# Twelve first-softmax maxima taken apart between ScalarE, GpSimd and VectorE, and some output matmuls moved between the fill pairs

## The chip, the cores and the metric

The kernel runs on one core of a Trainium2 chip. Its engines work side by side and meet at semaphores: TensorE (PE; its weight loads are listed apart as PEld), VectorE (DVE), ScalarE (ACT), GpSimd (POOL) and SyncE (SP, which here only issues DMAs). [...] The metric is the device time of one execution in microseconds; lower is better.

## The reference

An attention through 32 inducing points over 4 batches of 12416 rows of 128 values, and then a gated feed-forward layer on all 49664 rows:

```
def mab(q, kv):
    s = scale * (q @ kv.T)
    a = exp(s - s.max(-1))
    a /= a.sum(-1) + 1e-9
    return a @ kv
h = mab(inducing, x)        # first softmax: 32 rows over 12416 positions, per batch
y = mab(x, h)               # second softmax: 12416 rows over 32 positions, per batch
out = (sigmoid(y @ w_gate) * (y @ w_val)) @ w_out     # 128 -> 1536 -> 128
```

## The kernel before

**Shapes.** A batch is 97 pieces of 128 rows: six groups of 16 pieces and one piece alone. The hidden width of 1536 is 12 chunks `j` of 128. A block is four pieces (512 rows); one last block takes the four single pieces of the four batches. So there are 97 blocks of 12 chunks.

**The feed-forward layer.** The output of the second softmax is never formed. Its weights `a2` (32 per row) are multiplied at once with `hw = h @ w`, so a gate or value chunk is one matmul with 32 rows of contraction and 512 columns (a fill). Chunks go through *steps* of two and one chunks in turn; two steps are a *slot* of three chunks, and slots number the work of the whole kernel: 96 to a batch. In a step, `product(t)` (L964) has TensorE fill the values of step t and the gates of step t+2, and VectorE forms `u = (tanh + 1) * value` (L981); `gate(t + 2)` (L958) has ScalarE take tanh of the gates (L962). The PSUM tags are `g2, g1, v2, v1` (two- and one-chunk gates and values, one buffer each, six banks), `acc` and `m`. So the value fill of a step waits for VectorE's product two steps earlier, and the gate fill for ScalarE's tanh two steps earlier. `project` (L1050) sends output matmuls (L1062: 128 x 128, four a chunk) into `acc` from a queue, 12 a slot, or 16 while a block that starts with 24 or more waiting is under way; they stand at the end of the slot, behind both fill pairs. When a block is done ScalarE scales it into SBUF (L1081) and SP stores it.

**Beside it.** While batch b is in the feed-forward layer, the first softmax of batch b+1 and the second softmax of later groups run at slots that are written out by hand: `at(slot, make, late)` puts a piece of work behind the slot's first step (late False) or its second (late True), and `beside` (L1130) runs it. All of it shares the one PSUM bank `m`.

- First softmax, `plan_stage1` (L332), a group of 16 pieces: score matmuls into `m` (L255), the maximum over 512 columns by VectorE (L267), exponential by ScalarE one slot later (L280), transposition of the weights by a DMA on SP's queue, weighted sums on TensorE (L315) some slots later, and a copy of the sum (L330).
- `plan_combine` joins the seven groups of a batch with their maxima (GpSimd, with short VectorE and TensorE steps) and makes `hw`.
- Second softmax, `plan_stage2` (L617), a group: 16 small score matmuls into `m` (L483) in two slots, copy to SBUF by ScalarE (L520), `s2_lower_pool` on GpSimd (row maxima by a tree of subtract, clamp at zero, add: L530 to L532; then a subtraction, L535), exponential by ScalarE (L544), sums, inverse and spread on GpSimd (L552 to L598), and a DMA transposition.
- In the last batch nine chunks (`ASIDE`) bypass VectorE: gate and value are filled into `m` (L1015), ScalarE takes tanh and copies the value (L1025, L1029), and GpSimd forms the product (L1026, L1031). Their output matmuls stand at the end of their block.

Loads of x are issued on GpSimd's queue, their DMA transpositions, the output stores and the transpositions of weights on SP's. A prologue runs batch 0's first softmax before the loop.

Of the kernel before, what the change touches and what calls it, by code (L numbers as in the profile page):

```python
# [17 lines left out]
P = 128  # L18
GC = 16
BC = 4  # L20
ASIDE = {3: ((2, 9, 3, 8), (11, 17, 7, 1), (23, 26, 7, 0), (50, 53, 15, 3), (58, 62, 19, 11), (64, 69, 19, 10), (73, 76, 20, 5), (78, 81, 23, 11), (83, 88, 23, 10))}
LATE = (4, 19, 32, 46, 43)
# [15 lines left out]
def kernel(  # L38
# [31 lines left out]
    up = ctx.enter_context(tc.tile_pool(name="up", bufs=6))  # L70
    tp = ctx.enter_context(tc.tile_pool(name="tp", bufs=4))
    op = ctx.enter_context(tc.tile_pool(name="op", bufs=4))
# [145 lines left out]

    summed = [0] * B
    def keep_on(n, tag):  # L220
# [11 lines left out]
    def at(slot, make, late=False, side=False):  # L232
        plan.setdefault((slot, "side" if side else late), []).append(make)
# [15 lines left out]
    def s1_score_pe(b, s, tag, s1=None):  # L249
        c0, n = groups[s]  # L250
        ng, w, R = s1_dims(s)
        if s1 is None:
            s1 = ps.tile([P, 512], F32, tag=tag, name="s1_ps")
# [35 lines left out]
    def s1_turn_pe(b, s, a1T, tag="m"):  # L289
        ng, w, R = s1_dims(s)  # L290
        aT = ps.tile([P, 4, P], F16, tag=tag, name="aT_ps")
# [15 lines left out]
    def s1_sum_pe(b, s, a1, hp, k0, k1):  # L307
        c0, n = groups[s]
# [23 lines left out]
    def plan_stage1(b, s, score, total):  # L332
# [15 lines left out]
        at(score, begin)  # L348
        at(score + 1, weigh, late=full)
        at(score + 2, turn)  # L350
        first, second, keep = total

        def part(k0, k1):
            if k0 == 0:
                st["hp"] = ps.tile([P, C + 1], F32, tag="m", name="hp_ps")
# [4 lines left out]
        at(keep, lambda: s1_sum_keep(b, s, st["hp"]))  # L360
# [21 lines left out]
    def hw_fill(b, hf, tag):  # L382
        hw_ps = ps.tile([P, NI // 2, P], F32, tag=tag, name="hw_ps")
# [32 lines left out]
    def plan_combine(b, lead, weights, fill):  # L416
# [36 lines left out]
        def total():  # L453
            lh = ps.tile([P, 2, m], F32, tag="m", name="lh_ps")
# [4 lines left out]
        def part(hf):  # L459
            st["hw_ps"] = hw_fill(b, hf, "m")  # L460

        def keep(hf):
            if hf == 0:
                st["hwt"] = bp.tile([P, NI, P], F16, tag="hw", bufs=B, name="hwt")
            nc.scalar.copy(out=st["hwt"][:, ts(hf, NI // 2), :], in_=st["hw_ps"][:])
            if hf == 1:
# [724 lines left out]
```

## Time and profile before

| | before |
|---|---|
| median of 3 runs | 719.89 us (719.73 to 719.92) |
| span of the profiled execution | 718.4 us; the median is 1.5 us longer, for what lies around the span |
| mean granted TensorE clock | 0.999 |
| L267, maxima over 512 columns | 22 and 2 more, 683 ns each; six of them in the prologue |
| L962, tanh | 385 of 1024 columns at 1035 ns, 385 of 512 at 609 ns |
| L981, products | 385 of 1024 columns at 1214 ns, 384 of 512 at 679 ns |
| L280, exponentials of the first softmax | 22 at 683 ns and some smaller |

A row of the groups gives line, engine, operation, tiles, shapes and count, then busy time and mean duration of one, then the engine's idle time just before them and what ended it. Durations of neighbours on an engine overlap a little, so the spacing of starts is shorter than the mean duration.

### The profile page before, as it was taken

To read this page: it belongs to the slowest core of one execution; us is meant where nothing else is said; L and a number is where in the kernel's file an instruction comes from. 1 tells how busy PE (TensorE), PEld (TensorE's weight loads), DVE (VectorE), ACT (ScalarE), POOL (GpSimd) and SP (SyncE) were. 2 spreads that over 40 slices of the span, in tenths; PEclk is the share of its full clock that TensorE was granted. 3 is DMA by queue.
4 is the path that set the end of the run, shared out by engine and by line. 5 is a ranking of instruction groups with operands and counts; after the bars stand their busy time and mean duration, and the time that the engine had idled before them with its cause. 6 is when DMAs were issued, how large, how long until landed. Compare 5 with 4: busy or idle time off the path is not lost.

```text
span 718.4 us, 21566 instructions
## 1 busy us (share of the span) xinstructions
PE 650.5 (91%) x8446; PEld 394.2 (55%) x8446; DVE 702.4 (98%) x872; ACT 675.1 (94%) x1019; POOL 445.8 (62%) x718
## 2 busy tenths in 40 slices
PE   8889889999998998999989988999899999999897
PEld 4455555555555555555555555555555555555555
DVE  5899999999999999999999999999999999999997
ACT  4699999999999999999999999999999999999996
POOL 4574763888653747588666266387766787676220
PEclk9999999999999999999999999999999999999999
DMA  9796696244568344335268431220222122223011
GB/s 209 115 182 130 125 165 105 75 90 106 89 133 162 80 103 92 59 79 119 66 117 161 102 75 51 70 74 31 77 60 73 46 62 67 39 75 71 35 46 46
DMA packets 118182, 65.77 MB, mean 92 GB/s; under 512 B 101408, under 2 KB 102208, under 8 KB 118080
## 3 DMA queue, kind: packets, MB, share of 16 engines
q1 hardware_dynamic: 112176, 50.90, 31.6%
q0 software_dynamic: 5584, 13.34, 10.9%
q8 instruction: 66, 1.08, 0.6%
q14 instruction: 36, 0.29, 0.1%
q10 hardware_dynamic: 320, 0.15, 0.1%
HBM read 27.80 MB, written 25.43 MB: 74 GB/s over the span
## 4 chain that ended last, share of the span: by engine, by line
PE 51%; ACT 24%; DVE 16%; issue 5%; DMA 2%; DVEq 1%; POOL 1%; ACTq 0%
PE acc_ps L1062 24%; ACT t L962 22%; PE v_ps L944 21%; DVE u L981 14%; PE g_ps L944 2%; DMA xn<-in_x_dram 2%; PE s_ps L483 2%; PE hp_ps L315 1%; ACT o L1081 1%; DVE nm L267 1%; DVEq L981 1%; ACT a1T L280 0%; PE s_ps L255 0%; POOL xn L96 0%; ACTq L962 0%
## 5 line engine op out<-in xcount | busy, mean ns | idle before, releaser
L981 DVE SCALAR_TENSOR_TENSOR u<-t,v_ps 128x1024 f16<-128x1024 f16 (+1 forms) x771 | 670.9, 945 | 1.7 <-PE g_ps L944 0.8
L962 ACT ACTIVATE t<-g_ps 128x1024 f16<-128x1024 f32 (+1 forms) x770 | 589.5, 822 | 22.2 <-ACT t L962 10.3
L944 PE MATMUL v_ps<-a2r,hwt 32*128 32x512 f16 (+1 forms) x1179 | 290.8, 371 | 56.9 <-DVE u L981 53.2
L1062 PE MATMUL acc_ps<-wo,u 128*128 128x128 f16 x4620 | 324.5, 220 | 0.9
L1062 PEld LDWEIGHTS <-u 128*128 128x128 f16 x4620 | 259.9, 98 | 89.5 <-issue 88.1
L944 PE MATMUL g_ps<-a2r,hwt 32*128 32x512 f16 (+1 forms) x1179 | 294.0, 376 | 0.0
L944 PEld LDWEIGHTS <-hwt 32*128 32x128 f16 x2382 | 93.5, 91 | 188.6 <-issue 142.2
L552 POOL TENSOR_TENSOR sum<-e 128x256 f32<-128x256 f16 (+1 forms) x23 | 15.5, 672 | 133.8 <-ACT e L544 130.0
L598 POOL TENSOR_TENSOR a2n<-e,rs 128x2048 f16<-128x2048 f16 (+3 forms) x25 | 86.8, 3474 | 4.8 <-DVE rs L570 3.1
L576 POOL TENSOR_TENSOR near<-sme,minus 128x16 f32<-128x16 f32 (+1 forms) x22 | 65.3, 2966 | 1.8
L1081 ACT ACTIVATE o<-acc_ps 128x512 f32<-128x512 f32 x96 | 58.4, 609 | 0.0
L531 POOL TENSOR_SCALAR rise<-rise 128x256 f32<-128x256 f32 (+6 forms) x110 | 51.2, 466 | 9.7
L532 POOL TENSOR_TENSOR top<-top,rise 128x128 f32<-128x128 f32 (+3 forms) x88 | 28.4, 323 | 7.3
L552 POOL TENSOR_TENSOR sum<-sum 128x128 f32<-128x128 f32 (+3 forms) x92 | 28.4, 309 | 7.2
L530 POOL TENSOR_TENSOR rise<-top 128x128 f32<-128x128 f32 (+3 forms) x88 | 27.3, 310 | 6.9
L530 POOL TENSOR_TENSOR rise<-sc 128x256 f32<-128x256 f32 (+1 forms) x22 | 16.3, 739 | 20.9 <-ACT sc L520 20.6
L1031 POOL TENSOR_TENSOR xn_spare<-xn_spare 128x512 f16<-128x512 f32 x9 | 11.4, 1270 | 22.2 <-ACT xn_spare L1029 22.0
L535 POOL TENSOR_TENSOR sc<-sc,top 128x512 f32<-128x512 f32 (+1 forms) x22 | 23.9, 1086 | 1.7
L1026 POOL TENSOR_SCALAR xn_spare<-xn_spare 128x512 f32<-128x512 f16 x9 | 13.4, 1493 | 11.2 <-ACT xn_spare L1025 11.2
L483 PEld LDWEIGHTS <-xT 128*128 128x128 f16 x388 | 13.1, 96 | 11.7 <-issue 11.3
L280 ACT ACTIVATE a1T<-s_ps,nm 128x512 f16<-128x512 f32 (+1 forms) x26 | 16.4, 630 | 3.1 <-DVE nm L267 3.0
L483 PE MATMUL s_ps<-hT,xT 128*128 128x32 f16 x388 | 18.1, 178 | 0.1
(150 smaller groups left out, 291.4 us busy)
## 6 DMA issues: line engine op xcount, KB each, us to landing
out_dram<-o SPq DMA_DIRECT2D x96, 256.0 KB, 2.2
xn<-in_x_dram POOLq DMA_DIRECT2D x18, 512.0 KB, 7.7
xn<-in_x_dram POOLq DMA_DIRECT2D x3, 544.0 KB, 6.9
xn<-in_x_dram POOLq DMA_DIRECT2D x3, 256.0 KB, 12.8
xn<-in_x_dram SPq DMA_DIRECT2D x1, 576.0 KB, 4.8
xn<-in_x_dram SPq DMA_DIRECT2D x1, 512.0 KB, 3.9
a2r<-a2n SPq DMA_TRANSPOSE x29, 4.5
wg<-in_moe_w_gate_dram POOLq DMA_DIRECT2D x1, 384.0 KB, 12.7
```

Of the source, the lines that this page charges most:

```text
L483: nc.tensor.matmul(s2[:, j, :], xT[b][:, c + j, :], hT16[b][:], start=(j == 0), stop=whole and j == j1 - 1, skip_group_check=True,)
L530: nc.gpsimd.tensor_tensor(out=r, in0=far, in1=near, op=ALU.subtract)
L531: nc.gpsimd.tensor_scalar_max(out=r, in0=r, scalar1=0.0)
L532: nc.gpsimd.tensor_tensor(out=top[:, 0:n, 0:w], in0=near, in1=r, op=ALU.add)
L552: nc.gpsimd.tensor_tensor(out=d[:, 0:n, :], in0=src[:, :, 0:w], in1=src[:, :, w : 2 * w], op=ALU.add)
L576: nc.gpsimd.tensor_tensor(out=near[:, 0:n], in0=sme[:, 0:n], in1=minus1[:, 0:n], op=ALU.pow)
L598: eng.tensor_tensor(out=a2n[:, 0:n, :, :], in0=e.unsqueeze(2).to_broadcast((P, n, 4, m)), in1=rs.unsqueeze(2).unsqueeze(3).to_broadcast((P ...
L944: st[what + "end"] = nc.tensor.matmul(pt[:, k, col : col + nb * P], hw[b][r : r + 32, j // 2, :], a2r[r : r + 32, o : o + nb, :].rearrange ...
L962: st["tanh"] = nc.scalar.activation(out=st["t"][:], in_=st["g"][:], func=AF.Tanh, scale=0.5)
L981: u = nc.vector.scalar_tensor_tensor(out=st["u"][:, :, c:e], in0=st["t"][:, :, c:e], scalar=1.0, in1=st["v"][:, :, c:e], op0=ALU.add, op1= ...
L1062: nc.tensor.matmul(acc[0][(i // 2) % len(acc[0])][:, i, :], u[:, ts(i, P)], wo16[:, j, :], start=(i in fresh), stop=not any(e[2] == ib and ...
L1081: nc.scalar.mul(out=o32[:], in_=acc[0][0][:], mul=0.5)
```

## The change

**Maxima.** A first-softmax group whose row in the new table `TIMES` has two more slots goes another way. Its scores are filled into `m` at the first slot; late in the same slot ScalarE copies them negated to SBUF (`neg`) and GpSimd folds them by three levels of minimum (`lower_tree`: 512 to 256, 128, 64 columns, three instructions a level). At the second slot VectorE takes the minimum of the last 64 columns, at the third ScalarE takes the exponential from `neg` with scale -1. The other groups go as before. All slots of both softmaxes come from `TIMES` now (first batch, the two middle ones, last): many have moved by some slots, among them transposing loads of x for two groups to 15 and 12 slots before their batch.

**Output matmuls.** Behind the slot's first step, and so ahead of its second fill pair, up to three output matmuls (`GAP`; four in a block at the faster pace) are issued, if a block is under way and nothing else was put on TensorE in that slot so far. The slot still has 12, or 16 in the fast pace, which begins at 28 waiting (20 for blocks 81 and 93).

**The rest.** The chunks left out for the side path are always the last of their block, steps run across block ends, and four of the 18 side fills stand at other places in the slot. Buffers: `up` 6 to 4, `tp` and `op` 4 to 3, and a new pool for `neg`, `low` and the side tiles. The names `BEHIND`, `DROPPED` and `SWAP` are empty and switch nothing.

```
+GAP = 3
+BRISK = (81, 93)
+TIMES = (
+    {
+        "late": {2: (6, 7, 13, None), 3: (18, 19, 27, None), 4: (31, 33, 45, None), 5: (56, 57, 65, 52)},
+        "sum": ((10, 19, 22, 35, 35, 35), (13, 40, 41, 41), (25, 33, 37, 48, 49, 50), (37, 51, 51, 51), (42, 48, 49, 55, 55, 55), (45, 54, 54, 54), (22, 27, 27, 30)),
+        "join": (57, 61, (76, 78), (81, 83)),
+        "next": ((73, 74, 81), (86, 87, 94)),
+        "turn": (3, 7, 16, 21, 31, 37, 12),
+    },
+    {
+        "late": {2: (0, 3, 18, None), 3: (16, 21, 34, None), 4: (36, 37, 50, None), 5: (56, 57, 65, 52)},
+        "sum": ((9, 17, 17, 34, 35, 35), (13, 18, 26, 47, 48, 49), (-6, 3, 6, 50, 51, 51), (29, 35, 39, 45, 46, 46), (-3, 23, 24, 25), (31, 42, 42, 54, 55, 55), (39, 42, 43, 43)),
...
+        "turn": (0, 4, -15, 20, -12, 22, 30),
+    },
+    {
+        "late": {2: (4, 6, 14, None), 3: (19, 21, 29, None), 4: (32, 34, 42, None), 5: (46, 48, 56, 43)},
+    },
+)
+LOW = 64
...
+    def lower_tree(low, neg):
+        w, src = 2 * P, neg
+        rise1 = s2p.tile([P, (GC + NLO) * (m // 2)], F32, tag="sum16", name="rise1")
+        top1 = s2p.tile([P, (GC + NLO) * (m // 2)], F32, tag="sum16", name="top1")
+        while w >= LOW:
+            near, far = src[:, 0:w], src[:, w : 2 * w]
+            r = rise1[:, 0:w]
+            nc.gpsimd.tensor_tensor(out=r, in0=near, in1=far, op=ALU.subtract)
+            nc.gpsimd.tensor_scalar_max(out=r, in0=r, scalar1=0.0)
+            dst = low if w == LOW else top1
+            nc.gpsimd.tensor_tensor(out=dst[:, 0:w], in0=near, in1=r, op=ALU.subtract)
+            src = dst
+            w //= 2
...
+        def leave():
...
+            nc.scalar.mul(out=st["neg"][:], in_=st["s1"][:], mul=-1.0)
+            side_done()
+            lower_tree(st["low"], st["neg"])
+
+        def finish():
+            nm, _, col = s1_col(b, s)
+            nc.vector.tensor_reduce(
+                out=nm[:, col], in_=st["low"][:], axis=AX.X, op=ALU.min
+            )
...
+        if len(total) > 3:
+            done, weight, *total = total
+            at(score, fill)
+            at(score, leave, late=True)
+            at(done, finish)
+            at(weight, weigh_low, late=True)
+            at(weight + 1, turn)
...
         if t % 2 == 0:
             beside(t // 2, False)
+            early = 0
+            gap = BC if brisk or behind else GAP
+            if gap and acc[0] is not None and used == tensor_uses[0]:
+                early = len(queue)
+                project(t - 1, t, min(gap, waiting(t - 1) - 1, block_left() - 1))
+                early -= len(queue)
         else:
             beside(t // 2, True)
-            ready = waiting(t - 1)
+            room = 3 * BC - early if behind or not brisk else 3 * BC
             if acc[0] is None:
-                pace = 4 * BC if ready >= 6 * BC else 3 * BC
-            project(t - 1, t, pace)
+                brisk = waiting(t - 1) >= (5 if queue and queue[-1][2] in quick else 7) * BC
+                if brisk:
+                    room = 4 * BC
+            elif block_left() <= 4 * BC - early:
+                room = block_left()
+            project(t - 1, t, room)
```

A row of `"sum"` with six numbers has the slots of fill and copy, of the minimum, of the exponential, and three of the weighted sum; a row with four has one slot for score and maximum and the same three.

More of the change, by code (lines that the diff above doesn't have):

```diff
@@ L230, with at @@
     plan = {}
-    def at(slot, make, late=False, side=False):
-        plan.setdefault((slot, "side" if side else late), []).append(make)
+    def at(slot, make, late=False):
+        slot -= sum(d <= slot for d in DROPPED)
+        plan.setdefault((slot, late), []).append(make)
     def s1_col(b, s):
@@ L1084, in project @@
                 acc[0] = None
+                side_swap(now // 2)
                 if now < NST:
                     return
[L1089 removed]
     for b in range(B):
```

236 lines of the change are left out of this document (151 added, 85 removed).

## The prediction

> **What bounds the kernel now.** I read the page's first part, then who waits for whom, the stretches, the groups by shape, and at last the timeline of each engine around the places that the change touches. A "slot" is two steps of the main loop: three chunks, one two-chunk and one one-chunk product.
>
> ```profile
> span 718.4 us, 21566 instructions
> PE 650.5 (91%) x8446; PEld 394.2 (55%) x8446; DVE 702.4 (98%) x872; ACT 675.1 (94%) x1019; POOL 445.8 (62%) x718
> ...
> PE v_ps L944 <- DVE u L981: 54.1, 223, 0.8
> ACT t L962 <- ACT t L962: 10.3, 45, 0.5
> DVE u L981 <- PE g_ps L944: 0.8, 3, 0.3
> ...
> 130.00:180.00 50.00, 45.75 (x562) 27.68 (x559) 50.00 (x61) 48.26 (x73) 43.44 (x67) 1.00 0.40 92
> 180.00:230.00 50.00, 44.84 (x567) 27.04 (x566) 50.00 (x59) 47.88 (x69) 28.04 (x45) 1.00 0.69 128
> 430.00:480.00 50.00, 45.85 (x649) 28.18 (x646) 50.00 (x62) 48.61 (x78) 29.80 (x50) 1.00 0.20 57
> ```
>
> The stretches have busy time in the order PE, weight load, DVE, ACT, POOL. VectorE is busy for 50.00 of 50 us in each. It waited 0.8 us for TensorE in the whole run, and TensorE waited 54.1 us for VectorE. So VectorE sets the pace in the first three batches, and an instruction taken off it shortens the run by what it holds the engine, as long as ScalarE (48 to 49 of 50) and TensorE keep up. GpSimd has room on average: 28 to 43 of 50.
>
> How long VectorE needs for a slot, and how much of an instruction's mean time is its own, is read from the starts:
>
> ```profile
> 453.33 0.68 DVE L267 TENSOR_REDUCE nm<-s_ps 128x1 f32<-128x512 f32 x1
> 453.94 6.99 DVE L981 SCALAR_TENSOR_TENSOR u<-t,v_ps 128x512 f16<-128x512 f16 x8
> ...
> 467.85 19.10 DVE L981 SCALAR_TENSOR_TENSOR u<-t,v_ps 128x512 f16<-128x512 f16 x22
> 486.87 0.35 DVE L375 RECIPROCAL li<-lh_ps 128x32 f32<-128x32 f32 x1
> ...
> 578.23 107.18 DVE L981 SCALAR_TENSOR_TENSOR u<-t,v_ps 128x1024 f16<-128x1024 f16 x122 [0.22 <-PE g_ps L944]
> 685.69 26.23 DVE L981 SCALAR_TENSOR_TENSOR u<-t,v_ps 128x1024 f16<-128x1024 f16 x30 [0.27 <-PE g_ps L944]
> ```
>
> Twenty-two products, 11 slots, take 486.87 - 467.85 = 19.02 us: 1.729 us a slot. A maximum moves the next product by 453.94 - 453.33 = 0.61 us, though its own row says 0.68, since neighbours overlap by 0.07. In the last batch, which has no maxima, 122 products (61 slots) from 578.23 to 685.69 take 107.46 us, 1.762 a slot: 61 x 1.729 = 105.47, so 2.0 us are lost there, to something other than VectorE's own work.
>
> **The change, part by part.** *Thirteen maxima leave VectorE.* The rows with two slots more (a minimum's and an exponential's) are three in the first batch's list and five in the list used twice: 3 + 5 + 5 = 13, one more than the change's title says. Each drops a maximum over 512 columns and adds a minimum over 64. Groups by shape (the first row from the page), with busy us, mean ns, idle before:
>
> ```profile
> L981 DVE SCALAR_TENSOR_TENSOR u<-t,v_ps 128x1024 f16<-128x1024 f16 (+1 forms) x771 | 670.9, 945 | 1.7 <-PE g_ps L944 0.8
> ...
> L267 DVE TENSOR_REDUCE nm<-s_ps 128x1 f32<-128x512 f32 x22 | 15.0, 683 | 0.1
> L267 DVE TENSOR_REDUCE nm<-s_ps 32x1 f32<-32x128 f32 x4 | 1.1, 271 | 0.0
> L424 DVE TENSOR_REDUCE ml<-nm 128x1 f32<-128x7 f32 x3 | 0.5, 153 | 0.0
> L280 ACT ACTIVATE a1T<-s_ps,nm 128x512 f16<-128x512 f32 x22 | 15.0, 683 | 3.1 <-DVE nm L267 3.0
> L520 ACT COPY sc<-s_ps 128x512 f32<-128x512 f32 x22 | 13.1, 595 | 0.0
> ```
>
> Between 7 and 128 columns a reduction goes from 153 to 271 ns, so 64 columns are about 153 + 57/121 x 118 = 209 ns. The saving is 683 - 209 = 474 ns, the overlap being in both; 13 x 0.474 = **6.2 us**, all on the engine that sets the end.
>
> *ScalarE gets 13 copies,* and its 13 exponentials read SBUF in place of PSUM; I leave those at the row's 683. ScalarE's timeline:
>
> ```profile
> 442.70 0.59 ACT L520 COPY sc<-s_ps 128x512 f32<-128x512 f32 x1
> 443.17 3.09 ACT L962 ACTIVATE t<-g_ps 128x1024 f16<-128x1024 f32 x4
> 446.14 0.60 ACT L1081 ACTIVATE o<-acc_ps 128x512 f32<-128x512 f32 x1
> 446.62 1.57 ACT L962 ACTIVATE t<-g_ps 128x1024 f16<-128x1024 f32 x2
> 448.08 0.68 ACT L280 ACTIVATE a1T<-s_ps,nm 128x512 f16<-128x512 f32 x1
> 448.81 1.51 ACT L962 ACTIVATE t<-g_ps 128x1024 f16<-128x1024 f32 x2
> ```
>
> A copy moves the next tanh by 0.47 us, an output scaling by 0.48, an exponential by 0.73. Two slots of tanh take 446.14 - 443.17 = 2.97, 1.49 a slot against VectorE's 1.73: 0.24 spare. Four slots have 0.96 spare and mostly one output scaling, which leaves 0.48, so a copy is paid off in about four slots. In total ScalarE goes from 675.1 to about 675.1 + 13 x 0.47 = 681.2, VectorE from 702.4 to 696.2: VectorE stays the longer. But until now a maximum gave ScalarE 0.6 us just before each of these exponentials, and that cover goes. If a copy or exponential comes where ScalarE has no lead, the tanh behind it in its queue is late, and VectorE waits for that. Bounds: nothing (the 22 copies of L520 lie beside no maximum of their own, and all idle time ahead of the 771 products is 1.7 us), up to (0.47 - 0.24) + (0.73 - 0.24) = 0.72 for each, 9.4 us for 13. I take 0.08 each, **+1.0 us**, near the lower end, which is what the trace shows of the like.
>
> *GpSimd gets 13 trees* of three levels (256, 128, 64 columns; subtract, clamp, subtract), in the shapes that it already runs for the second softmax.
>
> ```profile
> 45.06 0.59 ACT L520 COPY sc<-s_ps 128x512 f32<-128x512 f32 x1
> ...
> 46.91 0.73 POOL L530 TENSOR_TENSOR rise<-sc 128x256 f32<-128x256 f32 x1
> ...
> 52.43 0.24 POOL L530 TENSOR_TENSOR rise<-top 128x32 f32<-128x32 f32 x1
> ...
> 54.46 1.08 POOL L535 TENSOR_TENSOR sc<-sc,top 128x512 f32<-128x512 f32 x1
> ...
> 66.11 0.66 POOL L552 TENSOR_TENSOR sum<-e 128x256 f32<-128x256 f16 x1 [10.02 <-ACT e L544]
> ...
> 72.66 3.61 POOL L598 TENSOR_TENSOR a2n<-e,rs 128x2048 f16<-128x2048 f16 x1
> ```
>
> The nine instructions from 46.91 up to 52.43 are such a tree: 5.5 us. A whole lowering of the second softmax is 54.46 + 1.08 - 46.91 = 8.6, its sums, inverse and spread 72.66 + 3.61 - 66.11 = 10.2. GpSimd's total rises by at most 13 x 5.5 = 72 us, to 518 of some 712. The minimum stands in VectorE's queue, so a late tree stops every product behind it. The tightest is group 1 of the later batches, copied at slot 13 and reduced at 18. From the lowering copied at slot -9 on, GpSimd's queue holds lowering, tree, sums and spread, lowering, tree, tree: 8.6 + 5.5 + 10.2 + 8.6 + 5.5 + 5.5 = 43.9 us or 25.4 slots. It starts about slot -8 (behind an earlier spread), ends about 17.4, and the minimum's turn comes at 18.65, behind that slot's large product: 2 us to spare. In the first batch the exponential of the second softmax's group 2 moves from slot 18 to 13: its lowering ended at 55.54, and six slots after the copy at 45.06 is 55.4, so ScalarE may wait some tenths once. I put **+0.2 us** for such places (0 to 2).
>
> *Moved DMAs.* Transposing loads of two groups go to slots -15 and -12, onto SP's queue, with output stores and the weight transposes behind them; each waits for an x load issued 6 slots (10 us) or more earlier. Cost nothing; if a load were later, stores would wait, and three output buffers cover three blocks, about 12 slots.
>
> *Three output matmuls between the fill pairs, and another pace in the last batch.*
>
> ```profile
> 503.86 0.84 PE L1062 MATMUL acc_ps<-wo,u 128*128 128x128 f16 x12
> 504.67 0.39 PE L944 MATMUL v_ps<-a2r,hwt 32*128 32x512 f16 x2
> ...
> 505.27 0.37 PE L944 MATMUL v_ps<-a2r,hwt 32*128 32x512 f16 x1 [0.18 <-DVE u L981]
> ...
> 601.57 1.07 PE L1062 MATMUL acc_ps<-wo,u 128*128 128x128 f16 x16
> 602.57 0.39 PE L944 MATMUL v_ps<-a2r,hwt 32*128 32x512 f16 x2
> ```
>
> TensorE idles 0.18 to 0.20 us in the slot, ahead of the one-chunk value fill; then 12 output matmuls run, and the two-chunk fill follows at once. Output matmuls come every (1.07 - 0.84)/4 = 0.06 to 0.07 us, so three fill that hole (0.2 us) and the group behind is shorter by as much. Where VectorE is in time this gains nothing: the value fill waits for VectorE anyway. Where a slot has 16 output matmuls or ScalarE is late, the two-chunk fill is late in the old order and VectorE waits. Counting the two pace rules through gives 8 slots of 16 before, all in the last batch; after, two plain ones and four with four of the 16 put into the hole. Of the 2.0 us lost between 578 and 686 I expect over half back: **-1.2 us** (0 to -2). At the end 24 output matmuls are left over in place of 16: 8 x 0.065 = 0.5 us, but they need only products that are done and run under the last two: nothing, at most +0.5.
>
> The sum: 718.4 - 6.2 + 1.0 + 0.2 - 1.2 = 712.2 for the profiled execution. The median of the runs shown, 719.89, lies 1.5 above the span, so **713.7 us**.
>
> **Rivals.** *Slower: ScalarE becomes the bound.* Place: the tanh behind each added copy and each exponential that has lost its maximum. Price: at the upper bound 9.4 in place of 1.0 us: 719.89 - 6.2 + 9.4 + 0.2 = 723.3, with the hole's gain also lost to ScalarE's lateness. It decides from 6.2/13 = 0.48 us a group. For it: ScalarE's 48 to 49 of 50. Against: 0.24 us spare in each slot, and the copies at L520 that broke nothing.
>
> *A smaller gain: GpSimd is late.* Were each tree 2 us later than reckoned where it is tight (six places), VectorE would wait for 2 to 4 us: 713.7 + 3 = 716.7. For it: 2 us to spare in the tightest place only by a long sum. Against: most minima stand six slots or more behind their copies.
>
> *No gain: GpSimd's added work slows VectorE itself.* If its 72 us held VectorE up for 9% of them (6.2/72), the saving would be gone: 719.9, or 718.7 with the pace's share. The products' rows in the two stretches above, GpSimd at 43.44 and then 28.04 of 50:
>
> ```profile
> L981 DVE SCALAR_TENSOR_TENSOR u<-t,v_ps 128x1024 f16<-128x1024 f16 x30 | 36.4, 1215 | 0.0
> L981 DVE SCALAR_TENSOR_TENSOR u<-t,v_ps 128x1024 f16<-128x1024 f16 x29 | 35.2, 1214 | 0.0
> ```
>
> One nanosecond for 15 us more of GpSimd: 30 products, 0.03 us; for 72 us that is 0.15. [...]
>
> *More: every stall of the last batch goes and none comes:* 719.89 - 6.2 - 2.0 - 0.3 = 711.4 (the last 30 products take 26.23 us, 15 x 1.729 is 25.94).
>
> **How the numbers follow.** The measurement tells 0.2% (1.4 us) from no change. The forecast, 712 to 715.5: 0.62. The larger gain, 711 to 712: 0.12. GpSimd late or part of ScalarE's price, 715.5 to 718.4: 0.12. No gain: 0.04. Slower: 0.10. Faster is 0.62 + 0.12 + 0.12 = 0.86. The range 711.0 to 717.0 takes in the forecast, the larger gain and the GpSimd case.
>
> **What would show it.** Right: a VectorE reduction of 128x64 x13 near 210 ns, 128x512 left with 11, VectorE about 696 us busy and unbroken, ScalarE about 681, GpSimd 505 to 518; output matmuls in groups of three and nine; the last batch's slots nearer 1.73. Wrong: VectorE waiting for the tree or for tanh by more than 2 us, products longer than 1214 ns, or a longer tail after the last product.

## The result, and the profile after

| | before | changed |
|---|---|---|
| median | 719.90 us (719.22 to 720.50, 15 runs) | 724.14 us (719.86 to 729.52, 15 runs) |
| ratio | | 1.006, 95% interval 1.0043 to 1.0077 |
| span of the profiled execution | 718.4 us | 718.1 us (its time 719.86, the shortest of the 15) |
| mean granted TensorE clock of the runs | 0.999 in the profiled run | 0.987 to 0.998 |

The forecast was 713.7 us and faster; the change is slower by 0.6%. The profiled execution is the fastest of the changed kernel, so about 4 us of what the median holds have to be looked for in another one (`changed_again`, below). An execution's time is 1.7 to 1.9 us above its span in every run of both kernels on record, so the 718.4 us of before belong to an execution some 0.3 us above the median. Three of the 110 runs of the kernel before on record were 3 to 4 us longer than its median too (722.96 to 724.23 us, clock 0.989 to 0.994), unprofiled and so of open cause.

In the changed kernel the products are L1096, tanh L1069, fills L1051, output matmuls L1194, output scaling L1213, old maxima L309, the short minimum L420, the negated copy L414 and its exponential L427, the first softmax's scores L297 and sums L359, the second's copies L624, the loads of x L122, their transposition L131 and the turn of the second softmax's weights L713.

The head of the page, and groups by shape:

```profile
span 718.1 us, 21727 instructions
PE 675.5 (94%) x8446; PEld 408.2 (57%) x8446; DVE 699.0 (97%) x872; ACT 678.1 (94%) x1032; POOL 506.9 (71%) x835
...
L1096 DVE SCALAR_TENSOR_TENSOR u<-t,v_ps 128x1024 f16<-128x1024 f16 x385 | 467.2, 1213 | 4.2 <-PE g_ps L1051 2.3
...
L309 DVE TENSOR_REDUCE nm<-s_ps 128x1 f32<-128x512 f32 x9 | 6.1, 685 | 1.4 <-PE s_ps L297 1.3
...
L420 DVE TENSOR_REDUCE nm<-low 128x1 f32<-128x64 f32 x13 | 2.7, 211 | 0.0
...
L427 ACT ACTIVATE a1T<-neg,nm 128x512 f16<-128x512 f32 x13 | 9.5, 733 | 0.0
L414 ACT ACTIVATE neg<-s_ps 128x512 f32<-128x512 f32 x13 | 8.1, 627 | 0.0
```

The maxima went as reckoned: 13 minima of 211 ns (209 forecast), no idle time ahead of them, so no tree was late; 9 maxima of L309 are left in this row, and 2 more go to another tile. Product rows are as long as before (1213 ns for 1024 columns, where the kernel before has 1214), with GpSimd at 71% in place of 62%. Yet the large products now have 4.2 us of idle time ahead of them, where all 771 had 1.7. The waits say where from:

```profile
PE v_ps L1051 <- DVE u L1096: 11.6, 52, 0.5
...
DVE u L1096 <- PE g_ps L1051: 2.3, 7, 0.7
PE s_ps L297 <- DMA xT<-xn: 2.1, 1, 2.1
...
DVE nm L309 <- PE s_ps L297: 1.3, 1, 1.3
```

TensorE's waiting for VectorE fell from 54.1 to 11.6 us. Most of that fall is not the maxima's: the output matmuls ahead of the second fill pair now stand where TensorE waited. With them alone in the kernel before (`before_gap`) the wait is 24.9 us, and without them `early_loads` (both below) goes from 11.7 to 35.9. And there is one new long wait, of scores for a transposed x. In stretches (busy PE, weight load, DVE, ACT, POOL, then the granted clock, DMA share, GB/s):

```profile
100.00:110.00 10.00, 9.76 (x144) 5.93 (x140) 10.00 (x12) 9.84 (x16) 7.11 (x16) 1.00 1.15 226
110.00:120.00 10.00, 7.65 (x87) 4.29 (x85) 7.42 (x10) 7.27 (x12) 7.25 (x14) 0.83 0.62 111
...
180.00:230.00 50.00, 47.38 (x557) 28.30 (x555) 49.73 (x59) 48.91 (x73) 43.34 (x74) 1.00 0.63 125
430.00:480.00 50.00, 48.34 (x711) 30.13 (x708) 49.62 (x62) 49.29 (x80) 37.49 (x67) 1.00 0.26 65
```

VectorE, unbroken before, loses 2.6 of 10 us from 110 to 120, and 0.3 to 0.4 of 50 in the two later stretches shown. From 110 to 120 the granted clock is 0.83; from 113.77 to 117.18 alone it is 0.50, so these are 3.4 us at half speed, as (1 - 0.83) x 10 / 0.5 gives too. The timeline there, TensorE first:

```profile
110.30 0.39 PE L1051 MATMUL g_ps<-a2r,hwt 32*128 32x512 f16 x2
112.82 0.40 PE L297 MATMUL s_ps<-xT,indT 128*32 128x512 f16 x4 [2.13 <-DMA xT<-xn]
...
114.64 0.60 PE L1051 MATMUL g_ps<-a2r,hwt 32*128 32x512 f16 x2
...
113.27 0.69 DVE L309 TENSOR_REDUCE nm<-s_ps 128x1 f32<-128x512 f32 x1 [1.30 <-PE s_ps L297]
...
115.28 1.82 DVE L1096 SCALAR_TENSOR_TENSOR u<-t,v_ps 128x1024 f16<-128x1024 f16 x2 [0.73 <-PE g_ps L1051]
117.65 2.95 DVE L1096 SCALAR_TENSOR_TENSOR u<-t,v_ps 128x1024 f16<-128x1024 f16 x3 [0.55 <-PE g_ps L1051]
```

The score matmuls of group 5 of the second batch stand at the head of TensorE's queue and wait 2.13 us; the fills behind them wait too; right after, fills take 0.60 in place of 0.39 us, and VectorE waits three times, 2.6 us in all. Why x is late is in the timelines of GpSimd and of SP's queue:

```profile
79.32 0.61 POOL L122 DMA_DIRECT2D xn<-in_x_dram  x1
79.96 0.74 POOL L383 TENSOR_TENSOR rise<-neg 128x256 f32<-128x256 f32 x1
...
85.44 0.67 POOL L656 TENSOR_TENSOR sum<-e 128x256 f32<-128x256 f16 x1
...
92.00 3.61 POOL L702 TENSOR_TENSOR a2n<-e,rs 128x2048 f16<-128x2048 f16 x1
95.55 1.18 POOL L122 DMA_DIRECT2D xn<-in_x_dram  x2
...
95.64 6.58 SPq L713 DMA_TRANSPOSE a2r<-a2n  x1
102.31 0.54 SPq L1215 DMA_DIRECT2D out_dram<-o  x1
102.94 3.99 SPq L131 DMA_TRANSPOSE xT<-xn  x1
```

Before, GpSimd was free early and issued three loads in one go:

```profile
84.78 1.71 POOL L96 DMA_DIRECT2D xn<-in_x_dram  x3
```

Loads are issued by GpSimd, in its order. Group 5's load for the second batch now stands behind a tree and behind the sums and the spread of another group, and goes out at 95.55, some 10 us later, together with the first load of the third batch; at the same time SP issues the turn of weights that the spread made ready, and behind it the transposition of group 5. Most of this is under way at the same time, and the mean share of the DMA engines from 100 to 110 is 1.15. The DMA view of 94 to 104 us gives size and time from issue to landing; the load of 544 KB is the third batch's (17 pieces), that of 512 KB is group 5's:

```profile
xn<-in_x_dram POOLq DMA_DIRECT2D x1, 544.0 KB, 8.8
xn<-in_x_dram POOLq DMA_DIRECT2D x1, 512.0 KB, 5.6
...
a2r<-a2n SPq DMA_TRANSPOSE x1, 10.9
xT<-xn SPq DMA_TRANSPOSE x1, 9.8
```

Issued at 102.94, the transposition lands 9.8 us later, at about 112.8; the scores start at 112.82. It did not wait for its own load, which had landed at 95.55 + 5.6 = 101.1, before the transposition was issued. What was still under way were the other load, pushed back behind it (to about 105.0), and the turn of weights (95.64 + 10.9 = 106.5).

### The profile page after: what moved, and what is told of

Its sections match the earlier page's. It is cut to its first block, busy times and chain, and to the rows that moved or that the text cites. A ratio compares the mean times of both kernels' runs of the same rounds, so it can differ in the third digit from the quotient of the medians.

```text
span 718.1 us, 21727 instructions
## 1 busy us (share of the span) xinstructions
PE 675.5 (94%) x8446; PEld 408.2 (57%) x8446; DVE 699.0 (97%) x872; ACT 678.1 (94%) x1032; POOL 506.9 (71%) x835
## 4 chain that ended last, share of the span: by engine, by line
PE 42%; DVE 24%; ACT 17%; POOL 8%; issue 5%; DMA 3%; DVEq 0%; ACTq 0%; SPq 0%; POOLq 0%
DVE u L1096 23%; PE acc_ps L1194 19%; PE v_ps L1051 17%; ACT t L1069 15%; PE g_ps L1051 3%; DMA xn<-in_x_dram 2%; DMA xT<-xn 1%; ACT o L1213 1%; PE s_ps L587 1%; POOL a2n L702 1%; PE hp_ps L359 1%; POOL rise L635 1%; POOL near L680 1%; POOL xn L122 1%; POOL top L636 1%
## 5 line engine op out<-in xcount | busy, mean ns | idle before, releaser
L1096 DVE SCALAR_TENSOR_TENSOR u<-t,v_ps 128x1024 f16<-128x1024 f16 (+1 forms) x771 | 673.4, 945 | 4.3 <-PE g_ps L1051 2.3
L1069 ACT ACTIVATE t<-g_ps 128x1024 f16<-128x1024 f32 (+1 forms) x770 | 591.2, 829 | 19.6 <-ACT t L1069 9.7
L1194 PE MATMUL acc_ps<-wo,u 128*128 128x128 f16 x4620 | 359.8, 221 | 1.7
L1194 PEld LDWEIGHTS <-u 128*128 128x128 f16 x4620 | 262.2, 98 | 135.0 <-issue 132.7
L1051 PE MATMUL v_ps<-a2r,hwt 32*128 32x512 f16 (+1 forms) x1179 | 294.0, 374 | 29.2 <-DVE u L1096 11.0
L1051 PE MATMUL g_ps<-a2r,hwt 32*128 32x512 f16 (+1 forms) x1179 | 295.0, 376 | 0.0
L1051 PEld LDWEIGHTS <-hwt 32*128 32x128 f16 x2382 | 105.8, 91 | 126.3 <-issue 42.2
L1213 ACT ACTIVATE o<-acc_ps 128x512 f32<-128x512 f32 x96 | 59.0, 615 | 0.2
L384 POOL TENSOR_SCALAR rise<-rise 128x256 f32<-128x256 f32 (+2 forms) x39 | 22.5, 577 | 3.4
L587 PEld LDWEIGHTS <-xT 128*128 128x128 f16 x388 | 13.1, 96 | 11.7 <-issue 11.3
```

Of the source, the lines that this page charges most:

```text
L587: nc.tensor.matmul(s2[:, j, :], xT[b][:, c + j, :], hT16[b][:], start=(j == 0), stop=whole and j == j1 - 1, skip_group_check=True,)
L1051: st[what + "end"] = nc.tensor.matmul(pt[:, k, col : col + nb * P], hw[b][r : r + 32, j // 2, :], a2r[r : r + 32, o : o + nb, :].rearrange ...
L1069: st["tanh"] = nc.scalar.activation(out=st["t"][:], in_=st["g"][:], func=AF.Tanh, scale=0.5)
L1096: u = nc.vector.scalar_tensor_tensor(out=st["u"][:, :, c:e], in0=st["t"][:, :, c:e], scalar=1.0, in1=st["v"][:, :, c:e], op0=ALU.add, op1= ...
L1194: nc.tensor.matmul(acc[0][(i // 2) % len(acc[0])][:, i, :], u[:, ts(i, P)], wo16[:, j, :], start=(i in fresh), stop=not any(e[2] == ib and ...
L1213: nc.scalar.mul(out=o32[:], in_=acc[0][0][:], mul=0.5)
```

## The experiments

A *VectorE stall* below is the spacing of the starts of two neighbouring VectorE instructions less what the first takes when nothing holds up the second (1131 ns for a two-chunk product, 598 for a one-chunk one, 600 for a full maximum, 126 to 129 for the short minimum). Summed over batches 0, 1 and 2 in the profiled executions it is 0.47 + 0.27 + 0.15 = 0.9 us before and 4.51 + 1.82 + 1.56 = 7.9 us after. That it goes from 13 x 0.601 to 13 x 0.129 us for the maxima, 6.1 us, is read from the same starts. Each expectation uses letters for theories in its own way.

**Theory: the late load makes the change slower, and what else is missing is ScalarE's.** First the loads of the second batch alone, issued earlier:

```
 # loads_only, against the changed kernel
-                at(o + (None, 4, 5, 17, 24, 31)[g], lambda g=g: x_load(1, g))
+                at(o + (None, 4, 5, 12, 17, 24)[g], lambda g=g: x_load(1, g))
```

> The changed kernel with the three x loads of the second batch earlier on GpSimd's queue, but the transposing loads at the changed kernel's own slots. If the wait comes from the load's place in GpSimd's queue, this does what both moves did: 717.6 us, no scatter. Rival: it comes from SP's queue, where the transposing load stands behind the turn of the second softmax's weights; then a wait of 1 us or more and some scatter remain, 719 to 723.

717.61 us (716.87 to 718.20), 0.9969 (0.9956 to 0.9981) of before. A load on GpSimd, the transposition on SP's queue, its landing, and the stretch:

```profile
80.39 0.61 POOL L122 DMA_DIRECT2D xn<-in_x_dram  x1
...
103.77 2.35 SPq L131 DMA_TRANSPOSE xT<-xn  x1
...
xT<-xn SPq DMA_TRANSPOSE x1, 4.5
...
110.00:120.00 10.00, 9.05 (x137) 5.81 (x135) 10.00 (x13) 9.79 (x16) 8.69 (x17) 1.00 0.70 129
```

The load goes out at 80.39. The transposition is issued no earlier than in the change (103.77), still behind the turn of weights, but lands after 4.5 us in place of 9.8: it was the load in its way, not its place in SP's queue. (The DMA engines' mean share from 100 to 110 is 1.09 here, so that share alone would not have told the two apart.) The wait is gone, the clock is 1.00, VectorE is unbroken from 110 to 120, and the scatter of the runs falls from 9.7 to 1.3 us. The late load cost 724.14 - 717.61 = 6.5 us in the median. `early_loads` moves the transpositions of these groups as well:

```
-        "turn": (3, 7, 16, 21, 31, 37, 12),
+        "turn": (3, 7, 16, 21, 28, 33, 12),
```

> The changed kernel with three x loads of the second batch issued 5 to 7 slots earlier on GpSimd's queue and two of its transposing loads 3 to 4 slots earlier on SP's; all else as changed. Theory A (the loss is a late transposing load, issued behind GpSimd's longer queue: TensorE waits 2 us for it, the granted clock halves for 3.4 us): that wait and the half-clock stretch go, the clock is 0.999, runs agree within 0.3%, and the time is 717 us (719.86 - 2.8). Rival B (the scatter of the runs, 719.9 to 729.5, comes from somewhere else, as from TensorE's denser work): the time stays near 724 and scatters as before.

717.58 us (716.83 to 718.11), 0.9972 (0.9961 to 0.9982): the same, so the earlier loads alone are enough. It is the base of several runs below.

`changed_again` is the changed kernel once more, for a profile of an execution near its median.

> The changed kernel once more, for a second profile. If a late transposing load of the second batch is the whole scatter, every half-clock stretch in it lies between 100 and 130 us from the start, behind a wait of TensorE, however long the run; a rival would show half-clock stretches elsewhere.

724.01 us, span 722.1. Its wait for x and two stretches:

```profile
PE s_ps L297 <- DMA xT<-xn: 2.3, 1, 2.3
...
110.00:120.00 10.00, 7.60 (x60) 3.97 (x58) 6.37 (x8) 6.41 (x10) 6.67 (x14) 0.65 0.60 114
120.00:130.00 10.00, 9.89 (x143) 6.19 (x142) 7.58 (x10) 7.73 (x13) 5.79 (x5) 0.67 0.20 54
```

The wait is 0.2 us longer, but the clock stays at half for 13.6 us ((0.35 + 0.33) x 10 / 0.5, with the 0.50 of the first profile) in place of 3.4, and the stalls of batch 0 are 8.2 us in place of 4.5. The whole stretch lies between 110 and 130 us, as the theory asked. That is the scatter, as far as these two profiles show it: a wait of about the same length, with a stretch at half clock of different length. Against `early_loads` (1.8 us in batch 0) it is 6.3 us, which is what the median lost.

`before_late_load` does to the kernel before what the longer queue did: one load is put five slots later, which has GpSimd issue it at 97.92 in place of about 86 us.

```
-                at(o + (None, 4, 5, 17, 24, 31)[g], lambda g=g: x_load(1, g))
+                at(o + (None, 4, 5, 17, 24, 36)[g], lambda g=g: x_load(1, g))
```

> The kernel before, with one x load (group 5 of the second batch) put from slot 31 to slot 36, so that GpSimd issues it behind the sums of a second softmax, about 97 us instead of 86 us after the start. Theory: TensorE then waits for its transposition near 110 us, the granted clock halves there, and the kernel before gets the changed one's fault: 721 to 724 us and a scatter of several us. Rival (the scatter needs the rest of the change): 719.9 with no scatter.

725.00 us (724.82 to 727.22), 1.0076 (1.0064 to 1.0089).

```profile
PE g_ps L944 <- DMA a2r<-a2n: 1.9, 1, 1.9
...
a2r<-a2n SPq DMA_TRANSPOSE x1, 12.3
...
120.00:130.00 10.00, 10.00 (x145) 6.13 (x143) 7.23 (x9) 7.94 (x15) 1.22 (x3) 0.66 0.07 28
```

The cost, 5.1 us against the runs of before beside it, is a little above the forecast (721 to 724), and comes by another door: here it is the turn of the second softmax's weights that lands late, 12.3 us after its issue where the kernel before has 9.7, and holds up a fill for 1.9 us; then come 6.8 us at half clock ((1 - 0.66) x 10 / 0.5). A late load alone is enough, with no tree in the kernel.

**What is left: 717.6 us where 713.7 were forecast.** `early_loads_old_maxima` keeps the slots of scores, sums and all else of `early_loads` and takes every maximum the old way, with its exponential one slot later.

```
-        if len(total) > 3:
-            done, weight, *total = total
...
-        else:
+        if True:
```

> The early loads, and the 13 maxima as before the change (VectorE over 512 columns of PSUM, exponential one slot later, no copy, no tree); slots and output matmuls as changed. VectorE has 13 x 0.47 = 6.1 us more. If the maxima's new way costs ScalarE and TensorE stalls of some 4 us (as the changed profile's batches suggest), this is only about 2 us slower than the early loads alone, 719; if the new way is free, 6 us slower, 723.

721.38 us (721.01 to 722.35), 1.0028 (1.0017 to 1.0039), with the buffers of the weights (pool `s1p`) raised from four to six. So in these slots the new way of the maxima is worth 721.38 - 717.58 = 3.8 us, and not 6.1: it gives back 2.3, 0.18 a group. Its stalls in batches 0 to 2 are 3.1 us, against 5.2 in `early_loads` and 0.9 before. So 2.2 of the 4.3 us of added stalls are there without a copy or a tree, and come with the moved slots.

`early_loads_no_gap` drops the output matmuls ahead of the second fill pair (`gap = 0`); `before_gap` puts only them into the kernel before.

> The same, without the output matmuls between the fill pairs (12 or 16 a slot, all behind the second pair). If the early matmuls do what was predicted (shorter group behind the second pair where ScalarE is late or 16 are due), the time is 1 to 3 us longer than with them, the stalls of the last batch growing from 2.5 towards 3 us. Rival: they cost TensorE switching time, and without them it is the same or shorter; if they are what disturbs the clock, the clock returns to 0.999 and the scatter goes here.

718.47 us (718.29 to 719.30), 0.9986 (0.9978 to 0.9995): they are worth 0.9 us there.

> The kernel before with only the early output matmuls added (three, or four in a fast block, ahead of the second fill pair, where the slot has nothing else on TensorE). Prediction's theory: 1.2 us less, all in the last batch, 718.7. Rival: no difference, 719.9, as VectorE sets the pace of the other batches and the last batch's stalls come from ScalarE. Rival: the early matmuls lose time by themselves, over 720.5, or scatter the runs.

719.27 us (718.67 to 719.78), 0.9996 (0.9987 to 1.0005): 0.4 us, and not told from none.

`double_copy` makes each of the 13 copies twice; `short_copy` makes them of 128 of the 512 columns, which GpSimd folds once and the exponential reads four times, so that the softmax of these groups leaves out three quarters of their columns. Both stand on `early_loads`.

```
 # double_copy: one line more
+            nc.scalar.mul(out=st["neg"][:], in_=st["s1"][:], mul=-1.0)
 # short_copy
-            nc.scalar.mul(out=st["neg"][:], in_=st["s1"][:], mul=-1.0)
+            nc.scalar.mul(out=st["neg"][:, 0:P], in_=st["s1"][:, 0:P], mul=-1.0)
```

> The kernel with early loads, each of the 13 negated copies made twice by ScalarE. If ScalarE's lateness makes the 1.5 us of stalls that each middle batch has beside its maxima, 13 x 0.47 us more of it cost at least half of that again and more: 717.6 + 3 to 5 = 721 to 723. Rival (TensorE's own extra matmuls make them, ScalarE has room): within 0.5 us of 717.6.

724.42 us (724.00 to 725.39), 1.0065 (1.0052 to 1.0077): 6.8 us more for about 13 x 0.47 = 6.1 us of ScalarE. Nothing of a second copy is hidden. Its waits name the path: TensorE's gate fills wait for tanh 13 times, 4.7 us in all, with the fills that VectorE needs behind them; `early_loads` has no such wait.

> The kernel with early loads, leaving work out: the 13 copies take 128 of 512 columns, GpSimd folds only the last level, and the exponential reads those 128 columns four times (so the softmax of these groups is that of a quarter of their columns). ScalarE has about 13 x 0.32 = 4.2 us less. If ScalarE's copies make the stalls, the middle batches' 1.5 us shrink to about 0.7 and the time is 715.5 us; if GpSimd's trees do (they shrink by two thirds too), the same, but then VectorE's waits are for the tree; if TensorE does, 717.6.

716.31 us (715.91 to 716.68), 0.9950 (0.9937 to 0.9962); the copy is 303 ns in place of 627, 13 x 0.32 = 4.2 us less for ScalarE, and 1.3 us are won; stalls in batches 0 to 2 fall from 5.2 to 3.8 us. The trees shrink here too, but no minimum waited for a tree in either run (idle time ahead of L420 is 0.0). So the first copy is mostly hidden and what lies on top of it is not: ScalarE is just at its edge. The stalls at slots 96, 182 and 186 (0.20, 0.13 and 0.17 us) stay as they were, so the copies' length does not make all of them.

Three attempts to get more, all on `loads_only`. `gates_behind` sets `BEHIND = (10, 86, 90, 96, 127, 182, 186, 223, 278)`, slots with the larger stalls, where both gate fills then go behind the second step; the switch also has ScalarE take the tanh of both later, and lets four output matmuls go early in place of three.

> The kernel with the earlier x loads, and in nine slots where VectorE was held up (10, 86, 90, 96, 127, 182, 186, 223, 278) the gate fill of the slot's first step is put behind the value fill of the second, so that TensorE does not stand at a gate fill that waits for tanh. If the stalls are ScalarE's lateness handed on by TensorE's order, these nine (1.6 us) shrink by more than half: 716.8 us. Rival: ScalarE itself is out of time there and the stall only moves: 717.6 or more.

720.53 us (719.86 to 721.12), 1.0010 (1.0001 to 1.0019): a miss; stalls went from 1.5, 1.8 and 1.6 to 2.4, 3.0 and 2.2 us. As three things moved at once, it does not tell which made it worse. `copies_later` puts nine scores with their copies one or two slots later (25 to 26 in the first batch; 9 to 10, 13 to 14, 29 to 30 and 31 to 33 in the two middle ones), and one minimum with them (18 to 19):

> The kernel with the earlier x loads, and nine of the 13 copies (fill, copy and tree) one slot later, two of them two, so that most no longer follow directly on an output scaling of ScalarE. If it is the bunching of ScalarE's extra work that costs, 0.5 to 1.5 us less: 716.5. Rival: ScalarE has no time to spare in any slot: 717.6.

718.38 us (718.00 to 719.75), 0.9979 (0.9966 to 0.9991): a miss, 0.8 us longer. `two_old` returns group 3 of the two middle batches to VectorE: `(29, 35, 39, 45, 46, 46)` becomes `(29, 45, 46, 46)`.

> The kernel with the earlier x loads, with one group (3) of each middle batch back to the maximum by VectorE: the copy of group 5 then stands behind that maximum. VectorE has 2 x 0.47 = 0.94 us more; if a copy bunched with another costs about as much as the maximum it saves, the time is within 0.4 us of 717.6; if the way of GpSimd is nearly free, 718.5; if it costs more than it saves, below 717.2.

717.82 us (717.04 to 718.25), 0.9970 (0.9959 to 0.9980): 0.2 us longer where 0.94 went back to VectorE, so each of these two trees had paid 0.1 us for its 0.47, less than the measurement resolves.

**Is it the moved slots or the maxima's new path?** `old_slots` is the changed code with the slots of before and no trees: `"sum": ((8, 15, 16, 17), (12, 18, 19, 19), (24, 31, 31, 31), ...)`. `old_slots_six_trees` sends groups 0, 1 and 2 of the two middle batches through copy, tree and minimum: `((8, 15, 15, 23, 23, 23), (12, 19, 19, 26, 27, 27), (24, 33, 33, 39, 39, 39), ...)`.

> The changed code with the slots of the kernel before: all maxima on VectorE, no copies and no trees; kept are only the output matmuls ahead of the fills in the last batch. If the moved slots made most of the remaining stalls (theory A), this run has VectorE stalls in batches 0 to 2 as before (0.9 us in all, 4.3 with the early loads) and takes 719.3 us, as before_gap did. If the changed code itself cost something apart from its slots (theory B), it takes over 720 us.

720.13 us (719.54 to 721.28), 1.0000 (0.9990 to 1.0009): between the two theories. The code around the slots, its fewer buffers included, costs nothing and, with the trees out, gains nothing that is measured.

> The same with six maxima, those of groups 0, 1 and 2 of the two middle batches, through copy, tree and short minimum; the slots of all else as before. VectorE is rid of 6 x 0.47 = 2.8 us. If the moved slots made most of the remaining stalls (theory A), a tree among the old slots costs little: 719.3 - 2.8 + 0.6 = 717.1 us. If the copies and the later exponentials make the stalls wherever they stand (theory C), each gives back about what the run with two old groups showed: over 718.5 us.

723.18 us (723.00 to 723.40), 1.0044 (1.0031 to 1.0058). The clock was 1.00. Six maxima less made it 3.1 us **longer**. Of these, 0.4 lie outside the span: a run's time is 2.2 us above its span in this kernel and the next two, and about 1.8 in all others; why is open. In the spans (medians 721.0 against 718.4) it is 2.6 us: VectorE was spared 2.8 and lost 5.4, 0.9 a group, nearly twice the saving; in the profile the stalls are 2.9 us more in batch 1 and 2.7 in batch 2. TensorE now waits for ScalarE, in two ways that `old_slots` does not have:

```profile
PE acc_ps L1194 <- ACT o L1213: 2.1, 6, 0.4
PE hp_ps L359 <- ACT sc L624: 2.0, 4, 0.6
```

ScalarE's and VectorE's timelines of the same work, first with the maximum (`old_slots`):

```profile
225.00 0.60 ACT L1213 ACTIVATE o<-acc_ps 128x512 f32<-128x512 f32 x1
...
224.68 0.68 DVE L309 TENSOR_REDUCE nm<-s_ps 128x1 f32<-128x512 f32 x1
225.28 4.14 DVE L1096 SCALAR_TENSOR_TENSOR u<-t,v_ps 128x512 f16<-128x512 f16 x5
```

and then with the tree (`old_slots_six_trees`, two rows of TensorE among them):

```profile
224.03 0.60 ACT L414 ACTIVATE neg<-s_ps 128x512 f32<-128x512 f32 x1
224.51 0.62 ACT L1213 ACTIVATE o<-acc_ps 128x512 f32<-128x512 f32 x1
224.99 4.20 ACT L1069 ACTIVATE t<-g_ps 128x1024 f16<-128x1024 f32 x5
...
225.18 0.83 PE L1194 MATMUL acc_ps<-wo,u 128*128 128x128 f16 x12 [0.34 <-ACT o L1213]
...
226.37 2.95 DVE L1096 SCALAR_TENSOR_TENSOR u<-t,v_ps 128x1024 f16<-128x1024 f16 x3 [0.25 <-PE v_ps L1051]
...
243.03 0.24 PE L359 MATMUL hp_ps<-xn,a 128*32 128x128 f16 x4 [0.57 <-ACT sc L624]
...
243.94 0.69 DVE L1096 SCALAR_TENSOR_TENSOR u<-t,v_ps 128x512 f16<-128x512 f16 x1 [0.20 <-ACT t L1069]
244.97 2.97 DVE L1096 SCALAR_TENSOR_TENSOR u<-t,v_ps 128x1024 f16<-128x1024 f16 x3 [0.35 <-PE g_ps L1051]
```

In the first, the maximum (0.60 us of VectorE) and the output scaling (0.48 us of ScalarE) lie side by side: each hides the other. The scaling comes every fourth slot, and the old slots of these maxima are multiples of four. In the second the maximum is gone and a copy stands in its place ahead of the scaling, 0.96 us of ScalarE together. The scaling ends later, the output matmuls wait 0.34 us for the bank `acc` that it empties, and the value fill of the next large product stands behind them in TensorE's queue. So it is at all three copies of a batch (slots 105, 109 and 121): 0.98 of the 2.9 us.

At 243 the sums wait 0.57 us for the bank `m` that the second softmax's copy L624 empties, and the value fill stands behind them; so it is at slots 119 and 135, 1.33 of the 2.9 us. This run's table puts the sums into the slot right behind that copy (23 and 39, behind 22 and 38), so this part is not the price of a tree as such, and the 0.9 a group is too high a price for one.

`old_slots_copies_apart` moves the six scores with their copies one slot on (9, 13, 25), off the scaling; `old_slots_copies_sums_apart` also takes the first group's sums from slot 23 to 23 and 24.

> The run with six trees among the old slots, with the scores and copies of those six groups one slot later (9, 13 and 25 in place of 8, 12 and 24), so that no copy stands directly ahead of ScalarE's output scaling, which comes every fourth slot. If ScalarE's run of copy and scaling is what makes VectorE wait there (theory D: 0.31, 0.33 and 0.34 us in each middle batch), the run is about 2 us shorter: 721.2 us. If a copy costs its stall wherever it stands, it stays at 723.2 us.

722.38 us (721.98 to 723.13), 1.0029 (1.0018 to 1.0040): 0.8 us won where 2 were expected. The six waits for the scaling are gone. The row of VectorE shows both that it works where it was aimed and, by the total, that the rest comes from elsewhere:

```profile
222.18 6.40 DVE L1096 SCALAR_TENSOR_TENSOR u<-t,v_ps 128x1024 f16<-128x1024 f16 x7
```

Seven products run in one piece over scaling and copy; the stalls of 0.31 and 0.33 us at slots 105 and 109 are gone, but the third copy's, 0.34 at 121, became 0.19 + 0.44 at 121 and 122, where sums now follow on the copy, and those at 117 to 119 and 131 to 135 stay, which follow exponentials and, at 119 and 135, the sums' wait for the copy L624.

> The same, and the weighted sums of the first group, 36 matmuls that all stood in slot 23 behind a copy of the second softmax, spread over slots 23 and 24. If the meeting of these with ScalarE's lateness made the 0.7 us of stalls at slots 118 and 119 (theory D), this takes another 1 us: 720.2 us. If it is the exponentials alone, it equals the run with the copies moved.

722.59 us (721.72 to 723.25), 1.0029 (1.0019 to 1.0040): a miss, as long as the one before. The sums' number in a slot isn't it; the first of them still stand in slot 23, and their four waits for the copy L624 are the same 2.0 us. Sums moved away from that copy were not tried.

## Why the prediction was wrong

**Failed: "Moved DMAs ... Cost nothing."** The argument looked at the transpositions that were moved and at SP's queue, and took from the old kernel that each load of x is issued six slots or more ahead. The loads of the second batch were not moved; but they stand in GpSimd's queue, and trees of 5.5 us and moved sums and spreads were put ahead of them. The part on GpSimd followed that queue for the minima and never for the DMAs in it, so it did not see a load go out 10 us later into the turn and the transposition. Nor was the load too late for its own transposition, the case that the prediction weighed; with the load out so late the transposition landed 9.8 us after its issue, and with the loads earlier (`loads_only`) after 4.5. Cost: 6.5 us in the median (`loads_only` against the change). TensorE's own wait is 2.1 to 2.3 us of it; the rest goes with the stretch at half clock, 3.4 us of it adding 3.0 us of stalls to batch 0 over `loads_only` and 13.6 us adding 6.7. Only "if a load were later, stores would wait" was said, and that wasn't the harm.

**Mis-sized: "13 ScalarE copies, +1.0", with "trees +0.2"; and no term for the moved slots.** Stalls in batches 0 to 2 rose by 4.3 us (0.9 to 5.2, `early_loads`) in place of 1.2: +3.1. As far as the runs part them, 2.2 of the 4.3 come with the moved slots alone (`early_loads_old_maxima`); in the medians it is 1.3 us, against `old_slots`, which has neither the early loads nor the two more buffers. The prediction had no term for them: its +0.2 is for late trees and one late exponential. The other 2.1, or 2.3 us in the medians, 0.18 a group, are the copies, trees and later exponentials, for which 1.2 was forecast.

The 0.08 a group was taken from copies that "lie beside no maximum of their own" and had broken nothing. That those copies were kept harmless by the maxima, which gave ScalarE 0.6 us every few slots, fits `old_slots_six_trees`, but is argued: no run takes a maximum away without adding a copy. There a group costs 0.9 us in the spans, and 0.77 with the copies moved ((2.8 + 1.8)/6); the whole forecast range was 0 to 0.72 each, and sums placed right behind another copy are part of that price. The path was only in part the one named, a late tanh: that is what `double_copy` shows, while among the old slots TensorE waits for the banks `acc` and `m`, which ScalarE empties late. So the places of the copies and sums decide whether a tree pays; with the old slots, as tried here, six of them lose.

**Mis-sized: "-1.2" for the last batch.** Its stalls went from 2.97 to 2.54 us; runs give 0.4 (`before_gap`) to 0.9 us (`early_loads_no_gap`). By the profile:

```profile
558.88 154.65 DVE L1096 SCALAR_TENSOR_TENSOR u<-t,v_ps 128x1024 f16<-128x1024 f16 x177
```

177 products, 88.5 slots, in 154.65 us are 1.747 a slot: half of the way from 1.762 to 1.729.

The sum is then 713.7 + 3.1 + 0.8 = 717.6, which is `early_loads` and `loads_only`; + 6.5 is the median of the change. The terms of batches 0 to 2 are read from one profile each, so that it meets the median to 0.1 us is partly luck.

**Right:** the 13 maxima and 6.1 us for them (6.2 forecast); no late tree; the end after the last product (713.53 to 718.1, 4.6 us, where it was 714.00 to 718.4, 4.4); PE's groups of three and nine. ScalarE is busy for 678.1 us (681 forecast), GpSimd for 506.9 (505 to 518). VectorE's 699.0 is 3 above the forecast 696.2; a likely reason is that busy time is a union of rows that overlap (a maximum's row is 685 ns, its spacing 600), and stalls take overlap away.

**The rivals.** That GpSimd slows VectorE didn't happen: products of 1024 columns are 1213 ns (1214 before) and a slot's two 1131 + 598 ns from start to start, as before, at 71% of GpSimd. The rival on the other side, ScalarE as the bound, was given 0.10 and 723.3 us; the change's median is near that number, but by luck: the late load made it. Its price is real in `double_copy` and, in part, in `old_slots_six_trees`.

The best version that ran with the whole computation is `loads_only`, or `early_loads`: 0.3% faster than before, both intervals below 1.

## What to carry to other kernels

When work is added to an engine's queue, go through everything that this engine issues behind it, DMAs too, and ask of each when it was issued before and who waits for its landing; the loads that a diff leaves alone can be moved all the same (here one went out at 95.55 in place of about 86 us, and loads issued earlier won 6.5 us back). An instruction on the bound engine can also be a pause for the others: before costing its removal, look at what runs beside it (here, 0.48 us of output scaling beside 0.60 us of maximum in the same slot), and take the price from the places where such pauses are missing, not from the average slack. Ask too what each added instruction puts off behind it: here it was often not the next tanh but the emptying of a PSUM bank for which TensorE stands, with VectorE's next fill behind (2.1 us of waits for `acc` and 2.0 for `m` in `old_slots_six_trees`). A kernel's scatter and granted clock are part of its profile: a median 4 us above the profiled execution calls for a second profile.

## What the runs showed of the hardware

The granted clock fell around a single pause of TensorE of about 2 us in each of the three profiles that hold one in the main loop: 2.13 us in the changed kernel (then 3.4 us at half clock), 2.28 in `changed_again` (13.6) and 1.9 in `before_late_load` (6.8). The 0.50 itself is read in the changed kernel, from 113.77 to 117.18; the other two lengths are worked out with it from means over 10 us. In the changed kernel the clock fell 0.95 us behind the end of the pause (112.82). In `changed_again` it fell before the pause was over: 7.0 us at half clock from 110 to 120, and more behind, put the fall at about 113.0 if the stretch is unbroken, and the pause ended at 113.49. In `before_late_load` it is 1.00 up to 120, and the turn of weights that TensorE waited for landed at about 118.8 (106.51 + 12.3), so it fell about 1.1 us or more behind the pause.

With shorter pauses the clock stayed up. In the kernel before the longest wait of TensorE in the loop is 0.78 us, in `loads_only` 0.5, and the clock is 1.00 from 35 to 714 us in the first and from 100 to 130 in the second. It is 1.00 in the prologue of the kernel before too (7 to 35), where TensorE once waits 1.45 us for x. In `before_late_load` that wait is 1.7 us, and by the sum it did nothing either: the mean clock of 0.994 is 8.7 us at half in a span of 723.2, of which 6.8 are the stretch above, and the kernel before has 2.0 at the end of its span (0.51 from 716.4 to 718.4). So in these profiles 1.9 to 2.3 us went with a fall and 1.7 or less did not. The stretches are 3.4 us and, to the rounding of the means, four times and twice as long; why they differ is open.
